# Turning q and k in 32x32 blocks on VectorE, and sink-attention rows in pairs

## The chip, the core and the metric

The kernel runs on one core of one Trainium2 chip. The time is the device time of one execution in microseconds; the figure used is the median of several executions. A profile is one further execution, recorded instruction by instruction. PE is the matrix engine (TensorE), DVE the VectorE, ACT the ScalarE, POOL the GpSimd; SP issues the transfers.

## The reference

Two attention layers follow each other, in float32. Shapes: 4 batches, 8 heads, 768 positions, head size 64.

```python
# first layer: every row sees the 4 first keys (sinks) and a window of 128
scores = scale * np.matmul(q, k.transpose(0, 1, 3, 2))
keep = is_sink | in_window
scores = np.where(keep, scores, -1e9)
a = softmax(scores);  x = (a @ v) -> [B, S, 512]
# second layer: four experts, causal attention each, top 2 of 4 by a gate
logits = x @ w_gate
for e in range(4):
    q, k, v = x @ wq[e], x @ wk[e], x @ wv[e]
    a = softmax(causal(scale * q @ k.T))
    out += gate_weight[e] * ((a @ v) @ wo[e])
```

`setup_inputs` draws q, k, v and the weights at random, with 4 sinks and a window of 128.

## The kernel before

The 768 positions are 6 blocks of 128. Work comes in units. A *first* unit is one batch and one pair of heads of the sink attention (`first`, then `band_rows`): 16 of them. A *second* unit is one batch and one pair of experts (`second`, then `wide_rows`): 8 of them. `values` makes the experts' values and the gate of a batch, `store` the output projection.

Every float32 operand of a large product is split into a high part (rounded to the fp32r type) and a low part (the rest), and each product is three matmuls: high·high, high·low, low·high.

A first unit goes as follows.

- q, k and v of two heads are loaded with positions on partitions (`load`, L712, two transfers for each tensor). The rings "qn" and "kn" have two buffers each.
- PE transposes q and k block by block into PSUM (`tr`, L729, 12 transposes of 128x128 per unit). `Pair.put` makes the parts: ACT copies the high part (L404), DVE subtracts for the low part (L408). q is scaled by -1/8 there. k's tile has 132 columns to a block: 128 keys, and 4 columns that repeat the sink keys, written by extra small instructions at L404 and L408.
- For each row block i, `scores` (L432) makes 260 columns for each of the two heads: the 128 keys of the block before, 4 sinks, the 128 keys of the block itself. The heads use the two halves of PE's rows. Each head has a PSUM bank of its own ("s", four buffers of one bank).
- For each head DVE adds a mask and takes the minimum of each row in one instruction (L632, the scores are negative-scaled, so the minimum is the largest score); ACT takes the exponential and the sum (L637); DVE adds 1e-9 and takes the reciprocal (`factor`, L468 and L469).
- In rows 2 to 5, POOL multiplies the sink columns by the factor (`keep`, L648), adds the two halves of the window into 128 columns, for in each row the halves hold complementary keys (`merge`, L656), and multiplies by the factor (`norm`, L663). Rows 0 and 1 are only multiplied.
- PE transposes the probabilities of two rows (L510; L486 for rows 0 and 1), DVE and ACT copy them out (L513 with a triangular mask, L356 or L358), and PE multiplies by the values (L453), by value differences and by the sinks (L457).

The order of all this is not the order of the code. Each piece is a `Step` with a priority, a cost by engine and what it waits for; `Plan.emit` places the steps one by one in a simulated time and emits the instructions in that order, so each engine's queue is fixed in advance. Priorities come from the place of the unit in a written list (`ORD` for a batch, `LAST` for the last: a number is a first unit of the batch, p a second unit of the batch before, c one of its own) and from leads and lags (`LEAD_S`, `PREP_1`, `AV_LAG` and others). `STAY` is a penalty on PE for changing between full-array, row-tiled (scores) and column-tiled (values) work.

Of the kernel before, what the change touches and what calls it, by code (L numbers as in the profile page):

```python
# [11 lines left out]
F32R = mybir.dt.float32r  # L12
AF = mybir.ActivationFunctionType
OP = mybir.AluOpType
# [15 lines left out]
STAY = 45.29  # L30
# [31 lines left out]
class Plan:  # L62
# [7 lines left out]
    def step(self, prio, cost, fn, after=(), new=(), use=(), fifo=None, moves=0, mode="full", behind=()):  # L70
        s = Step(prio, cost, fn, after, new, use, moves, mode, behind)
        if fifo is not None:
            self.fifo.setdefault(fifo, []).append(s)
        self.steps.append(s)
        return s
# [74 lines left out]
def kernel(  # L150
# [27 lines left out]
    none_kept = n_sink == 0 and window == 0  # L178

# [7 lines left out]
             "gate": 2, "gates": 1, "st": 6, "s": 4, "t": 3, "acc": 1}  # L187
# [21 lines left out]
    def window_mask(m, off, sinks):  # L209
        nc.gpsimd.affine_select(out=m, in_=m, pattern=[[-1, 128]], compare_op=OP.is_ge,  # L210
                                fill=-NEG, base=off, channel_multiplier=1)
        nc.gpsimd.affine_select(out=m, in_=m, pattern=[[1, 128]], compare_op=OP.is_ge,
                                fill=-NEG, base=window - 1 - off, channel_multiplier=-1)
# [6 lines left out]
    if banded:  # L220
        for i, ns in ((0, n_sink), (1, n_sink), (2, 0)):
            m = consts.tile([128, RW], F32, name=f"bmask{i}")
            nc.gpsimd.memset(m, 0.0)
            if i:
                window_mask(m[:, :128], 128, ns)
                if i == 1 or n_sink < 4:
                    nc.gpsimd.memset(m[:, 128 + (0 if i == 1 else n_sink):SW], -NEG)
            window_mask(m[:, SW:], 0, 0 if i else ns)
            for ii in range(i, NB if i == 2 else i + 1):
                row_mask[ii] = m  # L230

        own = consts.tile([128, 128], F32, name="own")
# [17 lines left out]
    else:  # L250
        for i in range(NB):
# [7 lines left out]
            if not none_kept:  # L259
                for c, j in enumerate(seen[i]):  # L260
# [5 lines left out]
                            compare_op=OP.is_ge, fill=-NEG, base=0, channel_multiplier=1)  # L266

    st_ring = [consts.tile([128, 5, 2], F32, name=f"st{n}") for n in range(rings["st"])]
# [93 lines left out]
    class Pair:  # L362
# [25 lines left out]
        def put(self, which, lo, hi, ps, t, prio, mul, after, kept=None):  # L388

            use, n, x = [t, self.tile(which)], (hi - lo) * 128, self.tile(which)  # L390
            sinks = which and self.ext and lo == 0
            if which == 0:
                cs = slice((lo - self.lo) * 128, (hi - self.lo) * 128)
                pieces = [(ps, lambda a: x.t[:, a, cs])]
            else:
                pieces = [(lambda: ps().rearrange("p (j c) -> p j c", c=128),
                           lambda a: self.k_at(x.t[:, a, :], slice(lo, hi), slice(0, 128)))]
                if sinks:
                    pieces.append((lambda: ps()[:, None, :4].to_broadcast([128, self.nk - 1, 4]),
                                   lambda a: self.k_at(x.t[:, a, :], slice(0, self.nk - 1), slice(128, SW))))  # L400

            def high():
                for src, dst in pieces:
                    nc.scalar.activation(dst(0), src(), AF.Copy, scale=mul)  # L404

            def low():
                for src, dst in pieces:
                    nc.vector.scalar_tensor_tensor(dst(1), src(), mul, dst(0).bitcast(F32), op0=OP.mult, op1=OP.subtract)  # L408
            some = 70 if sinks else 0
            h = plan.step(prio, {ACT: some + 60 + 0.833 * n}, high, after, (), use)  # L410
            steps = [h, plan.step(prio, {DVE: some * 1.3 + 70 + 1.04 * n}, low, [h], (), use)]
            if which and kept is not None:

                if sinks:
                    self.kept = plan.step(prio, {DVE: 70}, lambda: nc.vector.tensor_copy(kept, x.t[:, :, :4]), steps[:], (), [x])
                elif lo == self.k0:
                    def place():
# [540 lines left out]
```

## Time and profile before

| | |
|---|---|
| median of 3 runs | 441.64 us (440.98 to 441.94) |
| span of the profiled execution, first to last instruction | 438.3 us |
| that execution's own time | not listed apart from the three runs |
| mean granted clock of PE | 0.995 |
| transfers | 28.23 MB in 86,332 packets, 82,912 of them under 512 B |

The span leaves out what lies before the first and behind the last instruction. Engines work side by side, so their busy times do not add up; a busy share says how full an engine is, and the chain of work that ended last says which engine's work set the time. In a line of the groups there are: line of the code, engine, operation, output and inputs, shapes, count, then busy time in us, mean of one in ns, and the idle time just before them with what ended it.

### The profile page before, as it was taken

Reading aid. Unit: us, or ns where it says so; the run is one execution under the profiler, and the core shown is the slowest. Engines: PE = TensorE matmul, PEld = TensorE weight load, DVE = VectorE, ACT = ScalarE, POOL = GpSimd, SP = SyncE. Lnnn points to the kernel's source line nnn. Section 1 sums busy time; section 2 is a strip of 40 time slices with the busy share of each in tenths; the row PEclk is TensorE's granted clock in tenths of the full one; section 3 lists DMA queues with packets and bytes.
Section 4 is the critical chain, followed back from the end, with each engine's and each line's share of the span. In section 5 each row is a group of like instructions: output and inputs, shape, how many; then the busy total and the mean of one; then the engine's idle time right before and its main releaser. Section 6 shows DMA issues by size and latency. Waiting matters only on the chain.

```text
span 438.3 us, 11835 instructions
## 1 busy us (share of the span) xinstructions
PE 425.2 (97%) x4020; PEld 359.5 (82%) x4020; DVE 327.3 (75%) x1323; ACT 294.6 (67%) x910; POOL 271.1 (62%) x478
## 2 busy tenths in 40 slices
PE   8889999999999999999999999999999999999996
PEld 7568778988888888988888888898788788978874
DVE  3889986797769888559659988866967847455753
ACT  4989995477868868258768966864858747134650
POOL 8989999848638936437656856663655470073550
PEclk9989999999999999999999999999999999999999
DMA  8959771014005334013104426110000000021012
GB/s 169 229 116 180 159 158 38 2 37 109 2 1 110 92 110 126 2 26 83 40 1 82 90 67 173 28 37 1 1 1 2 1 2 1 18 79 50 2 49 97
DMA packets 86332, 28.23 MB, mean 64 GB/s; under 512 B 82912, under 2 KB 82912, under 8 KB 86272
## 3 DMA queue, kind: packets, MB, share of 16 engines
q1 hardware_dynamic: 86272, 27.48, 26.6%
q8 instruction: 32, 0.52, 0.5%
q14 instruction: 28, 0.23, 0.2%
HBM read 21.05 MB, written 6.29 MB: 62 GB/s over the span
## 4 chain that ended last, share of the span: by engine, by line
PE 81%; DVE 9%; ACT 4%; POOL 3%; issue 2%; POOLq 0%; ACTq 0%; DVEq 0%
PE acc L453 16%; PE s L432 15%; PE t L757 14%; PE t L486 11%; PE t L785 8%; PE t L831 8%; PE t L729 3%; PE t L510 3%; DVE p L632 2%; ACT pt L356 1%; PE acc L457 1%; DVE pt L513 1%; DVE p L568 1%; DVE ks L408 1%; PE t L516 1%
## 5 line engine op out<-in xcount | busy, mean ns | idle before, releaser
L637 ACT ACTIVATE p<-p,st 128x260 f32<-128x260 f32 (+1 forms) x192 | 93.6, 494 | 18.8 <-DVE st L632 14.8
L432 PE MATMUL s<-ks,qs 64*128 64x260 f32 (+4 forms) x960 | 92.0, 318 | 1.8 <-DVE st L632 0.8
L585 POOL TENSOR_TENSOR p<-p,st 128x128 f32<-128x128 f32 (+5 forms) x96 | 87.7, 936 | 3.1
L432 PEld LDWEIGHTS s<-ks,qs 64*128 64x128 f32 x960 | 69.1, 187 | 20.4 <-issue 10.4
L663 POOL TENSOR_TENSOR p<-p,st 128x256 f32<-128x256 f32 x96 | 65.4, 688 | 27.8 <-DVE st L469 18.2
L578 ACT ACTIVATE p<-p,st 128x384 f32<-128x384 f32 (+5 forms) x96 | 63.9, 668 | 23.1 <-DVE st L568 19.6
L632 DVE CUSTOM_DVE_ANT_0 p<-s,bmask 128x260 f32<-128x260 f32 (+1 forms) x192 | 69.8, 398 | 6.4 <-PE s L432 5.6
L356 ACT ACTIVATE pt<-t 128x512 f32<-128x512 f32 (+1 forms) x110 | 58.7, 544 | 20.1 <-PE t L486 10.6
L486 PE MATMUL t<-ident,p 128*128 128x128 f32 x432 | 63.2, 281 | 2.3 <-POOL p L663 0.7
L656 POOL TENSOR_TENSOR p<-p 128x256 f32<-128x256 f32 x64 | 46.6, 734 | 27.9 <-ACT p L637 27.5
L486 PEld LDWEIGHTS t<-ident,p 128*128 128x128 f32 x432 | 47.0, 141 | 10.8 <-issue 2.8
L568 DVE CUSTOM_DVE_ANT_0 p<-s,cmask 128x512 f32<-128x512 f32 (+3 forms) x96 | 50.8, 554 | 5.5 <-PE s L432 4.8
L472 POOL TENSOR_TENSOR st<-st,gate 128x2 f32<-128x2 f32 x48 | 9.4, 197 | 66.1 <-DVE st L469 39.2
L408 DVE SCALAR_TENSOR_TENSOR ks<-t,ks 128x384 fp32r<-128x384 f32 (+3 forms) x64 | 27.9, 456 | 19.9 <-ACT ks L404 19.6
L453 PE MATMUL acc<-pt,v 128*64 128x128 f32 x672 | 42.0, 276 | 0.0
L453 PE MATMUL acc<-pt,vn 128*64 128x128 f32 x448 | 40.7, 284 | 0.2 <-DVE x L344 0.2
L453 PEld LDWEIGHTS acc<-pt,v 128*64 128x64 f32 x672 | 36.2, 137 | 4.5 <-issue 2.2
L404 ACT ACTIVATE ks<-t 128x384 fp32r<-128x384 f32 (+3 forms) x64 | 24.8, 417 | 21.9 <-PE t L757 21.6
L637 ACT ACTIVATION_READ_ACCUMULATOR p<-p,st 128x1 f32 x192 | 38.0, 198 | 0.0
L468 DVE TENSOR_REDUCE st<-st 128x2 f32<-128x4 f32 x144 | 22.1, 154 | 20.5 <-ACT p L578 9.1
L785 PE MATMUL t<-wvh,x 128*128 128x260 f32 x192 | 36.7, 286 | 0.5 <-ACT pt L356 0.5
L408 DVE SCALAR_TENSOR_TENSOR qs<-t,qs 128x384 fp32r<-128x384 f32 (+2 forms) x48 | 26.4, 552 | 12.7 <-ACT qs L404 12.5
(103 smaller groups left out, 879.1 us busy)
## 6 DMA issues: line engine op xcount, KB each, us to landing
vn<-in_v_dram SPq DMA_DIRECT2D x32, 192.0 KB, 3.5
out_dram<-o SPq DMA_DIRECT2D x24, 256.0 KB, 2.0
qn<-in_q_dram SPq DMA_DIRECT2D x30, 192.0 KB, 4.3
kn<-in_k_dram SPq DMA_DIRECT2D x30, 192.0 KB, 4.3
o<-in_moe_wo_dram SPq DMA_DIRECT2D x2, 256.0 KB, 4.3
v<-in_moe_wv_dram SPq DMA_DIRECT2D x4, 128.0 KB, 4.1
v<-in_moe_wq_dram SPq DMA_DIRECT2D x4, 128.0 KB
v<-in_moe_wk_dram SPq DMA_DIRECT2D x4, 128.0 KB, 3.8
```

Of the source, the lines that this page charges most:

```text
L356: nc.scalar.activation(dst(), src(), AF.Copy)
L408: nc.vector.scalar_tensor_tensor(dst(1), src(), mul, dst(0).bitcast(F32), op0=OP.mult, op1=OP.subtract)
L432: nc.tensor.matmul(o, self.qs.t[hs, a, qs], self.ks.t[hs, b, ks], start=n == 0, stop=n == 2)
L453: nc.tensor.matmul(o[e * 64:e * 64 + 64], lhs, rhs, start=e not in self.begun, stop=last and i == self.hi - 1)
L486: nc.tensor.transpose(t.t[:, 2 * e + c, :], block(e, c), ident)
L578: nc.scalar.activation(x, x, AF.Exp, bias=st.t[:, 0, es], scale=-1.0, accum_out=st.t[:, 1, es])
L585: nc.gpsimd.tensor_mul(x, x, st.t[:, 2, e:e + 1].to_broadcast([128, n * 128]))
L632: nc.vector.tensor_tensor_reduce(out=p.t[:, e, a:], in0=s.t[:, a:RW], in1=row_mask[i][:, a:], scale=1.0, scalar=BIG, op0=OP.add, op1=OP.mi ...
L637: nc.scalar.activation(x, x, AF.Exp, bias=st.t[:, 0, e:e + 1], scale=-1.0, accum_out=st.t[:, 1, e:e + 1])
L663: nc.gpsimd.tensor_mul(x, x, st.t[:, 2, :][:, :, None].to_broadcast([128, 2, z - a]))
L757: nc.tensor.matmul(ps, w[a][:, c, es], X[b, c].t[:, x, cs], start=c == 0 and m == 0, stop=c == NCH - 1 and m == 2)
L785: nc.tensor.matmul(ps()[:, :VW], X[b, c].t[:, a, qs], W["wv"][w][:, c, :], start=c == 0 and n == 0, stop=c == NCH - 1 and n == 2)
```

## The change

For batches 1 to 3, q and k no longer go through PE. A transfer lays out each 32-column half of a head on 32 partitions, in runs of 32 numbers; DVE then transposes every 32x32 block in place, ACT copies the high part, and POOL subtracts for the low part. Batch 0 keeps PE's transposes. The scaling by -1/8 moves from q into the minimum instruction. The sink columns of k are placed by one POOL instruction for both parts.

In rows 2 to 5 the mask and the merge go. DVE copies, where a triangular predicate holds, the scores of the row's own block over those of the block before, in PSUM, for both heads at once; what remains is 132 columns, and the minimum runs over those with one mask for all these rows. Two rows share one tile of probabilities, one sum and reciprocal, one sink product and one norm. Both heads' scores are one PSUM buffer of two banks (ring "s": two buffers instead of four single ones).

The constants of the plan are set anew, the list of units among them.

```diff
+        def turn(self, which, lo, hi, src, nat, prio, after):
+            x, n = self.tile(which), (hi - lo) * 128
+            new, used = self.fresh(which)
+            part = lambda a: self.part(which, a, lo, hi)
+            turned = plan.step(prio, {DVE: 95 + 1.04 * n}, lambda: nc.vector.transpose(src(), src()), after, (), [nat])
+            h = plan.step(prio, {ACT: 95 + 0.833 * n}, lambda: nc.scalar.activation(part(0), src(), AF.Copy),
+                          [turned], new, [nat] + used, fifo=("qs", "ks")[which] if new else None)
+            def low():
+                nc.gpsimd.tensor_sub(part(1), src(), part(0).bitcast(F32))
...
+            def go():
+                nc.gpsimd.tensor_copy(self.k_at(self.ks.t, slice(0, self.nk - 1), slice(128, SW)),
+                                self.ks.t[:, :, None, :4].to_broadcast([128, 2, self.nk - 1, 4]))
...
+                        if which == 2 or by_pe:
+                            nc.sync.dma_start(t.t[:, a:z, e, :], x.rearrange("(t p) d -> p t d", p=128)[:, a:z, :])
+                            continue
+                        for h in range(2):
+                            to = t.t[64 * e + 32 * h:64 * e + 32 * h + 32].rearrange("p j e d -> p (j e d)")
+                            nc.sync.dma_start(to.rearrange("p (n c) -> p n c", c=32)[:, 4 * a:4 * z, :],
+                                              x.rearrange("(n r) (h c) -> h r n c", r=32, c=32)[h, :, 4 * a:4 * z, :])
...
+            def pick(s2=s2):
+                nc.vector.copy_predicated(s2.t[:, :, :128], earlier.bitcast(I32)[:, None, :].to_broadcast([128, 2, 128]), s2.t[:, :, SW:RW])
...
+                def low(e=e, n=n, s2=s2):
+                    nc.vector.tensor_tensor_reduce(out=p.t[:, n, :], in0=s2.t[:, e, :SW], in1=pair_mask, scale=-scale,
+                                                   scalar=BIG, op0=OP.add, op1=OP.min, accum_out=st.t[:, 0, n:n + 1])
...
-                def merge(p=p):
-                    nc.gpsimd.tensor_add(p.t[:, :, :128], p.t[:, :, :128], p.t[:, :, SW:])
...
+        r = factor(prio - LEAD_N, st, sums, w=4)
...
+        def norm():
+            nc.gpsimd.tensor_mul(p.t[:, :, :128], p.t[:, :, :128], f()[:, :, None].to_broadcast([128, 4, 128]))
...
-             "gate": 2, "gates": 1, "st": 6, "s": 4, "t": 3, "acc": 1}
+             "gate": 2, "gates": 1, "st": 6, "s": 2, "t": 3, "acc": 1}
-STAY = 45.29
+STAY = 32.79
-    LEAD_S, LEAD_E, LEAD_N = 9.9, 3.89, 4.91
-    WIDE_S, WIDE_E, WIDE_N = 10.54, 0.28, 6.11
-    UNIT_1, UNIT_2, AV_LAG = 11.19, 19.96, 4.12
+    LEAD_S, LEAD_E, LEAD_N = 11.81, 7.88, 6.72
+    WIDE_S, WIDE_E, WIDE_N = 10.9, 4.23, 6.32
+    UNIT_1, UNIT_2, AV_LAG = 12.14, 21.17, 7.72
-    ORD = "0 1 p0 2 p1 3"
-    LAST = "0 1 2 p0 3 p1 c0 c1"
+    ORD = "0 1 p0 p1 2 3"
+    LAST = "0 1 p0 3 2 p1 c0 c1"
-    PREP_0, PREP_1, PREP_2, VALUES, STORE = 11.25, 15.12, 10.77, 11.53, 6.72
-    WP, WS, LOAD_0, PREP_3, VALUES_0 = 11.14, 15.74, 34.09, 9.97, 11.15
+    PREP_0, PREP_1, PREP_2, VALUES, STORE = 19.49, 7.91, 17.67, 18.4, 13.2
+    WP, WS, LOAD_0, PREP_3, VALUES_0 = 10.42, 20.53, 37.8, 10.0, 11.15
```

More of the change, by code (lines that the diff above doesn't have):

```diff
@@ L409, in put @@
[L409 to L417, printed above, removed]
-                        copy = nc.vector.tensor_copy if to.eng == DVE else nc.gpsimd.tensor_copy
-                        copy(self.k_at(x.t, slice(self.k0, self.k0 + self.nk - 1), slice(128, SW)),
-                             kept[:, :, None, :].to_broadcast([128, 2, self.nk - 1, 4]))
-                    to = plan.step(prio, {DVE: 110, POOL: 220}, place, [h] + self.source, (), [x])
-                    steps.append(to)
@@ new lines, in turn_by_pe, with tr @@
+        def turn_by_pe(self, which, lo, hi, src, nat, prio, after):
+            t = new_t()
+            def tr():
+                for j in range(hi - lo):
+                    nc.tensor.transpose(t.t[:, j, :], src()[:, j, :], ident)
+            new, used = self.fresh(which)
+            tt = plan.step(prio, {PE: 109 * (hi - lo)}, tr, after, [t] + new, [nat] + used,
+                           fifo=("prep", ("qs", "ks")[which]) if new else "prep")
+            self.put(which, lo, hi, lambda: t.t[:, :hi - lo, :].rearrange("p c n -> p (c n)"), t, prio, [tt])
@@ L507, in tr @@
         def tr():
-            for r, p in enumerate(ps):
-                for e in range(2):
-                    nc.tensor.transpose(t.t[:, 2 * r + e, :], p.t[:, e, :128], ident)
-        tt = plan.step(prio, {PE: 436}, tr, normed, [t, whole, part], ps)
+            for n in range(4):
+                nc.tensor.transpose(t.t[:, n, :], p.t[:, n, :128], ident)
+        tt = plan.step(prio, {PE: 436}, tr, normed, [t, whole, part], [p])
         flat = lambda x: x.t.rearrange("p r e n -> p (r e) n")
@@ L549, in wide_rows @@
                 c1 = min(c0 + 4, n)
-                ss = [buf("s", [128, 512]) for _ in range(2)]
+                s2 = buf("s", [128, 2, 512])
                 runs = []
@@ L695, in over, with first @@
         return [x for a, b, steps in ready if a < hi and b > lo for x in steps]
-    def first(b, hp, groups, prio_of, prep_prio, load_prio, kept):
-        lo, hi = groups[0][0], groups[-1][1]
-        pair = Pair(banded, lo, hi)
-        whole = (b, hp, lo) == (0, 0, 0) and hi > 3
+    def first(b, hp, groups, prio_of, prep_prio, load_prio):
+        pair = Pair(banded)
+        whole, by_pe = (b, hp) == (0, 0), b == 0
         nat, loaded = [], []
@@ L714, in first @@
                 before = [x[2][0] for x in loaded[-1]]
                 loaded[-1].append((a, z, [plan.step(
-                    load_prio + (0.1 if n else 0.2 if which == 2 else 0), {SP: 950}, load, (), [] if n else [t], [t] if n else [],
-                    moves=364 * (z - a), behind=before, fifo=None if n else tag)]))
-        pair.source = KEPT.get(hp, []) if kept is not None else []
-        cuts = {w: [(a, min(a + 3, hi)) for a in range(lo if w == 0 else pair.k0, hi, 3)] for w in range(2)}
@@ L735, in first @@
-        if kept is not None and lo == 0:
-            KEPT[hp] = [pair.kept]
-        value = (lambda j, e: nat[2].t[:, j - pair.k0, e, :], lambda js: loaded[2][0][2], [nat[2]], pair.k0)
+                    load_prio + (0.1 if n else 0.2 if which == 2 else 0), {SP: 950 if which == 2 or by_pe else 1900}, load, (), [] if n else [t],
+                    [t] if n else [], moves=364 * (z - a), behind=before, fifo=None if n else tag)]))
+        for a, z in cut("0 3 6" if whole else TURNS):
+            for which in range(2):
+                t = nat[which]
+                (pair.turn_by_pe if by_pe else pair.turn)(which, a, z, lambda t=t, a=a, z=z: t.t[:, a:z].rearrange("p j e d -> p j (e d)"), t, prep_prio,
+                          over(loaded[which], a, z))
```

288 lines of the change are left out of this document (133 added, 155 removed).

## The prediction

> **What bounds the kernel now.** I read the page's first part, then the busy time in three stretches, then the chain of work that ended last in the first two of them.
>
> ```profile
> span 438.3 us, 11835 instructions
> PE 425.2 (97%) x4020; PEld 359.5 (82%) x4020; DVE 327.3 (75%) x1323; ACT 294.6 (67%) x910; POOL 271.1 (62%) x478
> ```
>
> ```profile
> core 0: us, PE busy (x) PEld busy (x) DVE busy (x) ACT busy (x) POOL busy (x), PEclk, DMA share, GB/s
> 0.00:60.00 60.00, 53.17 (x484) 42.05 (x484) 48.33 (x222) 50.15 (x174) 54.87 (x122) 0.97 0.81 169
> 60.00:420.00 360.00, 357.91 (x3437) 306.38 (x3436) 271.39 (x1089) 241.54 (x731) 212.87 (x354) 1.00 0.19 46
> ```
>
> The next two lines are the chain by line, of the stretch 60 to 420 us and of 0 to 60 us.
>
> ```profile
> by line: PE acc L453 19.0%; PE s L432 17.9%; PE t L757 17.1%; PE t L486 12.4%; PE t L785 9.8%; PE t L831 7.2%; PE t L729 3.5%; PE t L510 3.3%; PE acc L457 1.7%; issue 1.3%; DVE p L568 1.2%; PE t L516 0.9%; ACT pt L356 0.7%; DVE pt L513 0.6%
> ...
> by line: DVE p L632 10.2%; issue 9.1%; DVE pt L513 6.5%; PE s L432 5.3%; ACT pt L356 5.2%; DVE ks L408 5.0%; ACT p L637 4.7%; DVE x L344 3.7%; PE t L486 3.5%; DVE qs L408 3.4%; DVE pt L358 2.7%; ACT ks L404 2.7%; POOL p L663 2.6%; POOL bmas
> ```
>
> A busy PE proves little by itself, since its spans overlap; the chain does. From 60 to 420 us the PE entries add up to 92.8% of it (19.0+17.9+17.1+12.4+9.8+7.2+3.5+3.3+1.7+0.9), so a nanosecond of PE work taken out there is worth about a nanosecond. The other engines have room (DVE 271 of 360 us, POOL 213). The first 60 us are another regime: VectorE heads the chain, and POOL (54.9 of 60), ACT (50.2) and DVE (48.3) are all nearly full, because batch 0's four sink-attention units have no projections beside them. A cut of PE work there is worth nothing, and any DVE work added there is worth its price.
>
> **PE: what leaves.** The transposes of q and k are L729, 192 in all, of which batches 1 to 3 hold 12 pairs x 12 = 144. The second fence is the transposes by stretch; the third has pieces of the chain (start, duration, count).
>
> ```profile
> L729 PE MATMUL t<-ident,qn 128*128 128x128 f32 x96 | 16.8, 286 | 1.6 <-ACT pt L356 1.1 <-DVE pt L513 0.5
> L729 PE MATMUL t<-ident,kn 128*128 128x128 f32 x96 | 16.5, 282 | 0.1
> ```
>
> ```profile
> 0.00:60.00 60.00, 12.52 (x72) 9.02 (x72) 0.97 0.81 169
> 60.00:420.00 360.00, 16.79 (x120) 13.78 (x120) 1.00 0.19 46
> ```
>
> ```profile
> 105.87 0.87 PE t L486 x8
> ...
> 132.52 1.01 PE t L729 x9
> ```
>
> The mean of 286 ns is latency. Eight transposes that follow other full-array work occupy the chain for 0.87 us, 109 ns each; nine of L729 take 1.01 us, 112 ns each. So 120 x 0.109 = 13.1 us leave the stretch where PE is the chain (its 3.5% of 360 us, 12.6 us, says the same); the other 24 (2.6 us) leave the first 60 us and I count them at nothing. Scores, projections and P·V keep their matmuls.
>
> **DVE: what leaves and what comes.**
>
> ```profile
> L632 DVE CUSTOM_DVE_ANT_0 p<-s,bmask 128x260 f32<-128x260 f32 x160 | 62.6, 421 | 3.1 <-PE s L432 2.4
> L632 DVE CUSTOM_DVE_ANT_0 p<-s,bmask 128x128 f32<-128x128 f32 x32 | 8.7, 283 | 3.3 <-PE s L432 3.2
> L468 DVE TENSOR_REDUCE st<-st 128x2 f32<-128x4 f32 x144 | 22.1, 154 | 20.5 <-ACT p L578 9.1 <-ACT p L637 7.1 <-POOL p L656 1.9
> L469 DVE RECIPROCAL st<-st 128x2 f32<-128x2 f32 x144 | 23.9, 166 | 5.0
> L408 DVE SCALAR_TENSOR_TENSOR qs<-t,qs 128x384 fp32r<-128x384 f32 x32 | 17.6, 550 | 6.2 <-ACT qs L404 6.1
> L408 DVE SCALAR_TENSOR_TENSOR ks<-t,ks 128x20 fp32r<-128x20 f32 x16 | 2.7, 169 | 0.0
> L358 DVE COPY v<-t 128x256 f32<-128x256 f32 x18 | 7.6, 423 | 12.2 <-PE t L785 11.9 <-POOL p L656 0.3
> L358 DVE COPY pt<-t 128x512 f32<-128x512 f32 x35 | 23.7, 686 | 5.2 <-PE t L486 5.1
> ```
>
> Rows 2 to 5 of 16 pairs are 64 rows, so 128 masked minima shrink from 260 to 132 columns: 128 x (421-283) = -17.7 us. Two rows share one sum and reciprocal: -32 x (154+166) = -10.2. The 20-column sink copies go: -2.7. The low parts of 48 q/k groups go: -48 x 0.55 = -26.4. New are 48 in-place block transposes of 128x384, of which the trace has none. Their bounds are 0.42 us (the 256-column copy, if reading SBUF were much quicker) and 1.1 us (two passes of 0.55); I take one pass, 0.55, the row of the same size: +26.4 (20 to 53). New too are 64 predicated copies of 2x128 columns from PSUM to PSUM: 0.42 us if source and destination stream together (the 256-column copy), 0.69 if the old destination is streamed as well (the 512-column copy). I take 0.42, because only one side carries new data: +27.1 (to +43.9). The sum is -3.5 us, at worst +40, on 327. In the steady stretch that is hidden under PE; it costs wherever first-attention units stand side by side, since there DVE's order is minimum, factor and evacuation in one queue, and PE's next scores wait for a score tile to be freed. That tile now covers two banks, and both heads wait for the pick.
>
> The Trainium skill speaks against moving a transpose to this engine: by "VectorE: DVE Perf Modes", section "The three transpose paths", VectorE turns 32x32 blocks only and a 128x128 turn of bf16 takes 311 ns there. At 3 x 311 ns a group would take an estimated 0.93 us and the DVE sum would be about +15 us instead of -3.5; no run so far shows the instruction.
>
> **ACT and POOL.**
>
> ```profile
> L637 ACT ACTIVATE p<-p,st 128x260 f32<-128x260 f32 x160 | 81.1, 513 | 15.9 <-DVE st L632 12.0 <-POOL p L663 1.8 <-DVE gate L813 1.6
> L637 ACT ACTIVATE p<-p,st 128x128 f32<-128x128 f32 x32 | 12.6, 398 | 2.9 <-DVE st L632 2.9
> L656 POOL TENSOR_TENSOR p<-p 128x256 f32<-128x256 f32 x64 | 46.6, 734 | 27.9 <-ACT p L637 27.5
> L663 POOL TENSOR_TENSOR p<-p,st 128x256 f32<-128x256 f32 x80 | 48.7, 615 | 8.9 <-ACT p L637 5.0 <-PE t L486 3.5
> L648 POOL TENSOR_TENSOR psk<-p,st 128x24 f32<-128x24 f32 x64 | 14.2, 226 | 2.2 <-DVE st L469 1.4 <-DVE st L468 0.4
> L585 POOL TENSOR_TENSOR p<-p,st 128x512 f32<-128x512 f32 x16 | 16.4, 1046 | 0.2
> L585 POOL TENSOR_TENSOR p<-p,st 128x384 f32<-128x384 f32 x16 | 12.9, 828 | 0.5
> ```
>
> ACT: 128 exponentials lose 115 ns each, -14.7 us. POOL: the 64 merges go, -46.6; 64 sink products become 32, -7.2; 64 norms of 256 become 32 of 512, 33.5 for 39.4, -5.9. POOL gets 48 subtractions of 128x384, between 0.83 us (the product of that size) and 1.10 (1.5 times the merge, which reads two whole tiles); I take 1.0: +48. The 16 sink placements, 40 elements each, are nearest to the sink product: 16 x 0.23 = +3.7. Sum -8 us on 271. The k low part now waits in POOL's queue behind norms that PE's transposes wait for; 4 x 1.0 us per unit is covered as long as the preparation runs ahead.
>
> **The start.**
>
> ```profile
> 0.00:60.00 60.00, 11.64 (x16) 0.97 0.81 169
> ...
> 0.00:60.00 60.00, 20.26 (x110) 0.97 0.81 169
> ```
>
> The first line is the merges (L656), the second the minima (L632). In 0 to 60 us POOL loses 11.6 of merges, some 3 in norms and sink products, and gains 8 low parts (two pairs of batch 1): -7. ACT loses some 40 x 0.115 = 4.6. DVE stays level: 20 picks cost 8.4, 40 narrower minima and 10 factors save 8.7. The chain there is mostly DVE, so I take only -1 us, with +5 as the other end (the pick at 0.69 us adds 20 x 0.27 = 5.4) and -6 if POOL and ACT were the true holders.
>
> **DMA.** q and k of batches 1 to 3 come in runs of 32 numbers, 128 B instead of 256 B: twice the packets, 6144 per pair instead of 3072, from eight DMAs instead of four. The page of DMA for 100 to 120 us:
>
> ```profile
> DMA packets 4707, 1.22 MB, mean 61 GB/s; under 512 B 4704, under 2 KB 4704, under 8 KB 4704
> ...
> q1 hardware_dynamic: 4704, 1.18, 26.9%
> ...
> SPq L712 <- PE t L729: 95.0, 11, 28.3
> ```
>
> 26.9% of 16 engines x 20 us is 86 us for 4704 packets: 18.3 ns each. If a packet of half the size costs as much, a pair's q and k take 6144 x 18.3 / 16 = 7.0 us instead of 3.5; if the bytes decide, still 3.5. With a DMA share of 0.19 after 60 us this is hidden; in the first 60 us (0.81) two pairs add up to 7 us of transfers, which have some 11 us of empty DMA time there. The third line is SP's queue: loads already wait 95 us in all for L729 to give q/k buffers back, so they are issued as early as buffers allow. The buffer now goes free after POOL's low part, perhaps 3 us later per group.
>
> The Trainium skill, "DMA: Bandwidth & Descriptors", section "Why small descriptors are slow (HBM only)", gives a packet about 3 fixed cycles beside one per 32 B, so 11 cycles for 256 B and 7 for 128 B. From the measured 18.3 ns that is an estimated 11.6 ns, and 4.5 us per pair. Either way the transfer is hidden.
>
> **The sum.** 438.3 - 13.1 - 1 = 424.2 us of span. The median of the runs shown, 441.64, is 3.3 us above this span, and I keep that: 427.5. PE gets some waits back as it becomes faster than its feeders, and the order written out anew moves things both ways; I call it 427.
>
> **The rivals.**
> 1. *A larger gain, 420.* POOL and ACT hold the start, so it loses 6 us, and the 2.6 us of its PE transposes count in part: 441.6-13.1-6-2 = 420. For: POOL at 54.9 of 60 us. Against: DVE entries lead that chain.
> 2. *DVE takes over half, 436.* The pick at 0.69 us and the turn at 1.1: DVE +40 us, 367 in all. The start loses 5.4 us, and of the 13.1 PE gives back some 6 in waits for score tiles: 441.6-13.1+5.4+2 (turns of the first two pairs) = 436, up to 442. For: two PSUM operands in one instruction occur nowhere in this trace. Against: no DVE row here exceeds one pass.
> 3. *Slower, 448: the pick paces the first-attention units.* It sits between scores and minimum, and holds a two-bank score tile of which there are two. At a cost of 1.0 us, 0.58 over mine, 64 of them add 37 us to DVE; half of it on the path (the start, and the runs of first units, which the new order makes four long: 2, 3, 0, 1) is 18.5, so 441.6-14.1+18.5 = 446, and 2 for the turns. It decides from about 0.86 us a pick on, where half of 64 x 0.44 eats the 14.1 us.
> 4. *Loads come late, 445.* Each of the eight DMAs writes 32 partitions. Were only a quarter of the engines used, a pair's q and k would take 6144 x 18.3 / 4 = 28 us, and with two buffers each, four first units in a row at some 13 us each (55 minima in the first 60 us, 12 to a unit) would stand still some 6 us a batch, 18 in all: 441.6-14.1+18 = 445. It decides once a pair's load passes about 18 us. Against: the 256-byte loads already fill 0.81 of all 16 engines in the first 60 us.
>
> **How the numbers follow.** Forecast 0.52, larger gain 0.14, DVE half 0.21 (a quarter of it within 0.2% of before or above), pick 0.08, loads 0.05. The forecast's own range is 422 to 432 (the pick's and the turn's inner bounds, and the start from -3 to +3); the range for 8 in 10 runs from 416 to 438 and leaves out the two slower cases and the tail of the third. A measurement tells about 0.2% (0.9 us) from no change. Faster 0.82, same 0.05, slower 0.13.
>
> **What would show it.** The transposes' PE group falls to 48; the 60-to-420 chain stays over 90% PE, and that stretch's work ends 13 us sooner. The predicated copy at about 0.42 us, the block transpose at 0.55, POOL's subtraction at 1.0; POOL near 263 us, ACT near 280, DVE near 324. Packets rise by 36,864. I am wrong if a DVE row is above 0.7 us for the pick, if PE waits for DVE or for loads add up to more than 10 us after 60 us, or if the first units of batch 0 take longer than before.

## The result, and the profile after

The changed kernel takes 434.47 us (median of 4, 433.79 to 435.18) against 441.54 us (440.98 to 441.94) of the kernel before, run beside it: a ratio of 0.9842, 95% interval 0.9825 to 0.9858. It is faster by 7.1 us, a little less than half of the 14.5 us that were forecast. The profiled span fell from 438.3 to 432.4 us.

The page of the changed kernel: busy times, the granted clock in 40 slices, packets, and the chain of work that ended last.

```profile
span 432.4 us, 11450 instructions
PE 413.8 (96%) x3876; PEld 342.9 (79%) x3876; DVE 321.1 (74%) x1307; ACT 281.7 (65%) x894; POOL 265.0 (61%) x413
PEclk9699999999999999999999999999999999999999
...
q1 hardware_dynamic: 123904, 27.48, 30.1%
...
PE 72%; DVE 12%; ACT 5%; POOL 5%; issue 3%; DMA 2%; SPq 0%; POOLq 0%; DVEq 0%; ACTq 0%
```

The same two lines of the kernel before:

```profile
PEclk9989999999999999999999999999999999999999
...
PE 81%; DVE 9%; ACT 4%; POOL 3%; issue 2%; POOLq 0%; ACTq 0%; DVEq 0%
```

The side engines came out within 3 us of the forecast (DVE 321.1 for 324, ACT 281.7 for 280, POOL 265.0 for 263). What moved is the chain: PE holds 72% of it instead of 81%, and DVE, ACT, POOL, issue and DMA have taken 9 points more. The groups of the changed kernel, by line and shape, show that the price of each new instruction was right:

```profile
L703 DVE CUSTOM_DVE_ANT_0 p<-s,pair_mask 128x132 f32<-128x132 f32 x128 | 32.6, 287 | 0.5
L696 DVE COPY_PREDICATED s<-earlier,s 128x256 f32<-128x256 int32 x64 | 25.5, 421 | 1.4 <-PE s L463 1.4
L451 POOL TENSOR_TENSOR qs<-qn,qs 128x384 fp32r<-128x384 f32 x24 | 24.2, 1013 | 16.2 <-ACT qs L447 16.2
L446 DVE STREAM_TRANSPOSE kn<-kn 128x384 f32<-128x384 f32 x24 | 13.2, 562 | 0.1
L446 DVE STREAM_TRANSPOSE qn<-qn 128x384 f32<-128x384 f32 x24 | 12.8, 557 | 0.1
L434 PE MATMUL t<-ident,kn 128*128 128x128 f32 x24 | 4.8, 318 | 1.0 <-DVE ks L411 1.0
L434 PE MATMUL t<-ident,qn 128*128 128x128 f32 x24 | 4.5, 298 | 0.1
```

A pick takes 0.421 us (0.42 forecast), a turn 0.56 (0.55), GpSimd's low part 1.01 (1.0), and 48 transposes are left on PE. So the missing 7.4 us are not in a price. Two views say where to look. First the chain of the changed kernel from 60 to 420 us, by line, where the kernel before had 92.8% PE:

```profile
by line: PE t L794 17.2%; PE acc L484 16.5%; PE s L463 14.6%; PE t L517 11.0%; PE t L822 10.0%; PE t L868 6.8%; PE t L540 2.8%; issue 1.9%; PE acc L488 1.6%; DVE p L598 1.5%; DVE pt L543 1.4%; DVE pt L365 1.2%; ACT p L608 1.2%; ACT pt L363 
```

The PE entries that can be seen add up to 80.5%. Then the busy times of the two stretches:

```profile
0.00:60.00 60.00, 50.35 (x472) 39.66 (x474) 46.35 (x209) 47.37 (x165) 49.92 (x104) 0.94 0.82 162
60.00:420.00 360.00, 355.11 (x3353) 296.99 (x3350) 270.20 (x1092) 233.60 (x729) 215.06 (x310) 1.00 0.22 48
```

PE still looks 98.6% busy after 60 us (355.11 of 360), because the spans of matmuls overlap and short waits vanish inside them. To see those waits I counted from the starts of the matmuls in the trace: each at the distance at which its kind follows itself when packed (109 ns for a transpose, columns divided by 2.4 plus 8 to 14 ns for longer ones, half of it where two share the array), 94 to 149 ns for each change between full-array, row-tiled and column-tiled work, and the rest, time at half clock included, as waiting. By this estimate, in us from the first matmul to the last:

| kernel | packed PE work | changes of tiling | waiting | of it after 60 us |
|---|---|---|---|---|
| before | 368.0 | 33.2 | 31.9 | 15.3 |
| changed | 352.3 | 34.9 | 39.6 | 21.2 |
| difference | -15.7 | +1.7 | +7.7 | +5.9 |

15.7 us of PE work went out, as 144 x 0.109, and 9.4 us came back as waits and changes: -6.3 us, which is the fall of the span (5.9) with 0.4 us more ahead of the first matmul and behind the last. The experiments ask what these waits are.

### The profile page after: what moved, and what is told of

Same layout as the page of the kernel before. It is cut to its first block, busy times and chain, and to the rows that moved or that the text cites. A ratio compares the mean times of both kernels' runs of the same rounds, so it can differ in the third digit from the quotient of the medians.

```text
span 432.4 us, 11450 instructions
## 1 busy us (share of the span) xinstructions
PE 413.8 (96%) x3876; PEld 342.9 (79%) x3876; DVE 321.1 (74%) x1307; ACT 281.7 (65%) x894; POOL 265.0 (61%) x413
## 4 chain that ended last, share of the span: by engine, by line
PE 72%; DVE 12%; ACT 5%; POOL 5%; issue 3%; DMA 2%; SPq 0%; POOLq 0%; DVEq 0%; ACTq 0%
PE acc L484 15%; PE t L794 14%; PE s L463 13%; PE t L517 10%; PE t L822 8%; PE t L868 6%; PE t L540 3%; ACT pt L363 2%; DVE pt L543 2%; PE acc L488 1%; DVE p L598 1%; DVE p L703 1%; DVE s L696 1%; DVE pt L365 1%; ACT p L608 1%
## 5 line engine op out<-in xcount | busy, mean ns | idle before, releaser
L608 ACT ACTIVATE p<-p,st 128x128 f32<-128x128 f32 (+5 forms) x96 | 63.6, 664 | 18.5 <-DVE st L598 16.3
L707 ACT ACTIVATE p<-p,st 128x132 f32<-128x132 f32 x128 | 50.5, 398 | 12.3 <-DVE st L703 10.5
L365 DVE COPY pt<-t 128x512 f32<-128x512 f32 (+1 forms) x54 | 32.0, 596 | 7.5 <-PE t L517 7.2
L716 POOL TENSOR_TENSOR psk<-p,st 128x48 f32<-128x48 f32 x32 | 8.6, 268 | 43.3 <-DVE st L500 31.9
L868 PE MATMUL t<-woh,y 128*128 128x512 f32 x96 | 34.7, 412 | 0.0
L451 POOL TENSOR_TENSOR qs<-qn,qs 128x384 fp32r<-128x384 f32 x24 | 24.2, 1013 | 16.2 <-ACT qs L447 16.2
L722 POOL TENSOR_TENSOR p<-p,st 128x512 f32<-128x512 f32 x32 | 33.4, 1042 | 0.1
L703 DVE CUSTOM_DVE_ANT_0 p<-s,pair_mask 128x132 f32<-128x132 f32 x128 | 32.6, 287 | 0.5
L794 PE MATMUL t<-x,wqh 128*128 128x256 f32 (+1 forms) x128 | 32.7, 344 | 0.0
L794 PE MATMUL t<-x,wkh 128*128 128x256 f32 (+1 forms) x128 | 32.1, 340 | 0.4 <-DVE qs L411 0.4
```

The lines of the kernel that those rows point to most:

```text
L608: nc.scalar.activation(x, x, AF.Exp, bias=st.t[:, 0, es], scale=-1.0, accum_out=st.t[:, 1, es])
L703: nc.vector.tensor_tensor_reduce(out=p.t[:, n, :], in0=s2.t[:, e, :SW], in1=pair_mask, scale=-scale, scalar=BIG, op0=OP.add, op1=OP.min, a ...
L707: nc.scalar.activation(p.t[:, n, :], p.t[:, n, :], AF.Exp, bias=st.t[:, 0, n:n + 1], scale=-1.0, accum_out=st.t[:, 1, n:n + 1])
L794: nc.tensor.matmul(ps, w[a][:, c, es], X[b, c].t[:, x, cs], start=c == 0 and m == 0, stop=c == NCH - 1 and m == 2)
L868: nc.tensor.matmul(ps(), Y[b, c].t[:, a, qs], W["wo"][w][:, c, :], start=c == 0 and n == 0, stop=c == EP - 1 and n == 2)
```

## The experiments

Theory one: behind PE stands a second path, only a few us shorter, and less PE work uncovers it. Rivals: one part of the change is dearer than it looks, the new order is bad, or the loads are late.

**Less and more PE work, nothing else changed.** In the kernel before, batches 1 to 3 make one of three q and k transposes and use its result three times (e1); then they make each of them twice (e5).

```diff
-                    for j in range(a, z):
+                    for j in range(a, z if b == 0 else a + 1):      # e1_pe_light
+                    for j in [x for x in range(a, z) for _ in range(2 if b else 1)]:   # e5_pe_heavy
```

> The kernel before, with its order untouched, but in batches 1 to 3 only one of three q/k transposes is made and its result is copied three times (96 of 144 transposes left out, the numbers of q and k in those batches are not the right ones). Nothing is added to any engine. 80 of the 96 lie past 60 us: 80 x 0.109 = 8.7 us of PE work. Theory A (past 60 us PE time is worth its length; the changed kernel loses the rest because VectorE, GpSimd and the loads got new work): 441.5 - 8.7 = 433, at most 434.5. Theory B (in an order fixed ahead, PE meets the softmax path of other engines again and again, so freed PE time mostly turns into waits whatever is added): 437 to 440.

Measured: 438.68 us against 441.38, ratio 0.9944 (0.9925 to 0.9964). Of the 10.5 us taken out, 2.7 are had.

> The kernel before, order untouched, but each of the 144 q/k transposes of batches 1 to 3 is made twice into the same place (15.7 us more PE work, the same numbers; 13.1 us of it past 60 us). The mirror of the run that took 96 of them out and gained 2.5 us of 8.7. If PE is the slowest path with only a thin margin over the next one, adding is not symmetric to taking away: 441.4 + 13.1 = 454.5, at least 452. If the gain was small because PE time there simply lies in gaps of the order, adding should cost as little as taking away gained: 444 to 446.

Measured: 454.14 us against 441.61, ratio 1.0277 (1.0251 to 1.0303). Of 15.7 us put in, 12.5 are paid. The chains by engine, first of e1, then of e5:

```profile
PE 77%; DVE 13%; ACT 5%; issue 3%; POOL 1%; ACTq 0%; POOLq 0%; DVEq 0%
```

```profile
PE 86%; DVE 5%; POOL 4%; ACT 2%; issue 2%; POOLq 0%; ACTq 0%; DVEq 0%
```

Up, a nanosecond of PE work costs 0.8; down, it is worth 0.26. If only the transposes past 60 us are counted, 13.1 us put in and 8.7 taken out, the figures are 0.95 and 0.31. In the count above e1's waiting rises from 31.9 to 39.6 us, as much as in the changed kernel. This needs none of the new instructions. It is what a second path of nearly the same length does; which work makes up that path, these two runs do not show.

**Is it only the order?** An order written for longer PE work might hide the gain. e13 gives the work of e1 constants searched for it, e10 gives the kernel before new constants and nothing else.

```diff
-                tt = plan.step(prep_prio, {PE: 109 * (z - a)}, tr, ...
+                tt = plan.step(prep_prio, {PE: 109 * (z - a if b == 0 else 1)}, tr, ...   # e13_light_tuned
-    LAST = "0 1 2 p0 3 p1 c0 c1"
+    LAST = "0 2 1 p0 3 p1 c0 c1"                                     # e13 and e10_before_tuned
-    PREP_0, PREP_1, PREP_2, VALUES, STORE = 11.25, 15.12, 10.77, 11.53, 6.72
+    PREP_0, PREP_1, PREP_2, VALUES, STORE = 12.56, 15.25, 9.91, 15.32, 6.78   # e10; leads and lags likewise
```

> e1_pe_light's work (the kernel before, in batches 1 to 3 one of three q and k transposes, its result used three times), but the planner is told of the shorter TensorE step and the constants are searched anew for it. Theory one (behind TensorE stands a second path, only a few us shorter, whatever the order): new constants add at most 2 us to e1's gain, 436.5 to 438.5 us. Theory two (only the order, written for the longer work, hides the rest of the 10.5 us): with an order of its own the gain comes nanosecond for nanosecond, 431 to 433 us.

> The kernel before with none of the change's work, its constants of the schedule searched anew by the same planner (the plan grows shorter by 0.74 us of 428.7). Theory one (the new work made room that new constants then use; constants alone give the old work nothing): within 1 us of the kernel before, 440.5 to 442. Rival (the kernel before was merely badly scheduled, and any new order gives those 7 us): 435 to 437 us.

Measured: e13 440.73 us against 441.63, ratio 0.9981 (0.9969 to 0.9992); e10 442.55 against 441.94, ratio 1.0017 (1.0 to 1.0033). Theory two of e13 falls: an order made for the lighter work brought less on the chip than e1's old order. Theory one gave 436.5 to 438.5 and missed too, on the other side. Constants alone give the old work nothing.

**The parts alone, and the parts with the old constants.** e2 has only the turn, GpSimd's low parts and the 128-byte loads, e11 only the picked rows in pairs; e3 is the whole change with the old constants and list.

```diff
+                if b:                                                # e2_turn_before, in the kernel before
+                    pair.turn(which, a, z, ...)
+                    continue
-        whole, by_pe = (b, hp) == (0, 0), b == 0
+        whole, by_pe = (b, hp) == (0, 0), True                       # e11_rows_before, and the old constants
-    ORD = "0 1 p0 p1 2 3"
+    ORD = "0 1 p0 2 p1 3"                                            # e3_old_consts; all other constants likewise
```

> The kernel before with only the turn of q and k on VectorE, low parts on GpSimd and the 128 B loads (scale moved into the minimum as in the changed kernel); rows single, merges kept, constants and list of units as before. PE loses 15.7 us, GpSimd gains some 52 us (48 x 1.01 + 16 x 0.22) and stands near 320 of 440. Theory A: PE's 13.1 us come out less what GpSimd takes back, 430 to 436. Theory B: 436 to 442, no better than half of the 13.1 us. A third, that GpSimd's extra 52 us are what the row pairs had to pay for: slower than before, over 442.

> The kernel before with the picked rows and the row pairs alone: every batch's q and k are turned by TensorE and split as before, the loads are the old ones, and the constants are the old ones. VectorE then gets the 64 copies of 0.42 us and the 2 x 132 minimum in place of 260 wide ones on top of its old low parts. Theory one (a pick on the way from scores to exponentials costs its latency, and VectorE, relieved of no low parts, queues): slower than before by 4 to 10 us, 446 to 452. Rival (the shorter minima, exponentials and paired row ends are the part that pays, and the turn adds nothing): 434 to 438 us.

> The changed kernel with the constants and the list of units of the kernel before (units 0 1 p0 2 p1 3, leads, lags and the mode penalty as before). All work is the changed kernel's. Theory A (work sets the time): within 2 us of 434.5. Theory B (the order sets how much of the freed PE time is kept): 438 to 443, the larger part of the 7 us gone.

Measured: e2 457.12 us against 441.38, ratio 1.0364 (1.0324 to 1.0403); e11 451.64 against 441.94, ratio 1.0224 (1.018 to 1.0269); e3 441.54 against 441.38, ratio 1.0001 (0.9979 to 1.0024). Busy times, first of e2, then of e11:

```profile
PE 425.3 (93%) x3876; PEld 351.8 (77%) x3876; DVE 337.2 (74%) x1315; ACT 290.4 (64%) x894; POOL 317.4 (69%) x538
```

```profile
PE 431.3 (96%) x4020; PEld 360.5 (80%) x4020; DVE 324.8 (72%) x1313; ACT 280.4 (62%) x888; POOL 219.5 (49%) x365
```

POOL is the last number: 271 us in the kernel before, 317 with the turn alone, 219 with the pairs alone. Each part alone, with the old constants, makes the kernel slower by 10 to 16 us. For e2 a part of this can be seen in the trace: a small gate instruction on DVE (the three times are its shortest, median and longest, in ns), and PE's wait behind it.

```profile
L842 DVE TENSOR_TENSOR gates<-gate x4: 246/249/8710, 95.0 to 399.4; 128x96 f32<-128x96 f32 x4
```

```profile
105.83 0.48 PE L459 MATMUL s<-ks,qs 64*128 64x128 f32 x2 [5.79 <-ACT ks L405]
```

The instruction took 8.71 us instead of 0.25 once, from 94.98 to 103.69 us, while GpSimd worked 8.60 us of these 8.71; the gate, a copy of k on ACT and PE's next scores stood behind it, and PE waited 5.79 us. That GpSimd's work held it up was not tested. e2 also spends six to eight stretches of 3.41 us at half clock, the kernel before one to four (the last section has the price). What makes e11 slow was not shown: its DVE is busy 324.8 us, no more than the 327.3 of the kernel before. Together the parts come out even, and the new constants bring the 7 us. With the old constants no part has a gain of its own; constants searched for one part alone were not tried.

**Other orders of the changed kernel.** e7 has other constants with the same unit list, e8 other constants and lists. In e8 three first units stand side by side between batches 1 and 2, where the changed kernel has four, but five between batches 2 and 3.

```diff
-    LEAD_S, LEAD_E, LEAD_N = 11.81, 7.88, 6.72
+    LEAD_S, LEAD_E, LEAD_N = 11.38, 7.35, 6.13                       # e7_order_a; others likewise
-    ORD = "0 1 p0 p1 2 3"
+    ORD = "0 1 p0 3 p1 2"                                            # e8_order_b; others likewise
-    LAST = "0 1 p0 3 2 p1 c0 c1"
+    LAST = "1 0 2 3 p0 p1 c0 c1"                                     # e8_order_b
```

> The changed kernel with the same instructions and the same list of units; only constants of the plan differ (leads, lags, places, the mode penalty, and two costs of the plan set to what the trace measured: GpSimd's low part 1.0 us, the sink placement 0.22), so the instructions stand in another order on each engine. If the order decides how much of the 15.7 us is kept, another order moves the time by several us with all work unchanged, and this one was chosen to be tighter: 429 to 433. If the work decides, within 1 us of 434.5.

> As the run before, with other constants and the units listed as 0 1 p0 3 p1 2, in the last batch 1 0 2 3 p0 p1 c0 c1: all four first units of the last batch stand side by side, while elsewhere no more than three do. If the order decides: 429 to 434. If the work decides: within 1 us of 434.5. If runs of four first units are the weak place, it is no slower than the order before it.

Measured: 434.12 us (ratio 0.9833, 0.9807 to 0.9859) and 434.77 us (0.9836, 0.981 to 0.9862), both the same as the changed kernel. Three orders that differ much end within 0.7 us of each other; the old constants (e3) end 7 us later with the same work.

**The suspects, one at a time.** All in the changed kernel's own order: the block transposes left out (e4), the predicated copies left out (e6), the old 256-byte loads (e12, with as many transfers as the changed kernel, so it tests the size of the packets alone).

```diff
-            turned = plan.step(prio, {DVE: 95 + 1.04 * n}, lambda: nc.vector.transpose(src(), src()), after, (), [nat])
+            turned = plan.step(prio, {DVE: 95 + 1.04 * n}, lambda: None, after, (), [nat])        # e4_no_turn
-                nc.vector.copy_predicated(s2.t[:, :, :128], earlier.bitcast(I32)[:, None, :].to_broadcast([128, 2, 128]), s2.t[:, :, SW:RW])
+                return                                                                              # e6_no_pick
-                            nc.sync.dma_start(to.rearrange("p (n c) -> p n c", c=32)[:, 4 * a:4 * z, :], ...
+                            nc.sync.dma_start(t.t[:, js, e, :], x.rearrange("(t p) d -> p t d", p=128)[:, js, :])   # e12_plain_load
```

> The changed kernel in its own order, but the 48 block transposes on VectorE are left out (q and k of batches 1 to 3 go on unturned, so the numbers are not the right ones): VectorE loses 48 x 0.56 = 27 us. Theory A with the turns as the cost: 434.5 falls by 5 to 8 us, to 427 to 429. Theory B: PE does not wait for the turns but for order and latency: 432 to 434.5.

> The changed kernel in its own order without the 64 predicated copies (the own block's scores are not brought over, so the probabilities are not the right ones). VectorE loses 64 x 0.42 = 27 us, as much as without the turns (which gave 0.7 us), but this time on the path from scores to exponential. If the softmax path of single rows is what PE waits for: 434.5 falls by 3 to 6 us. If PE waits for no single operation but for the order as a whole: 433 to 434.5.

> The changed kernel in the same order, but q and k of batches 1 to 3 are fetched in the old 256-byte rows instead of 128-byte pieces: half as many packets there, two issues in place of four. The block transposes then leave q and k not transposed as the products need them; all times of other instructions stay. Theory one (the loads lie behind other work): within 0.5 us of the changed kernel, 434.0 to 435.0 us. Rival (packets compete with the moe loads, and issues on SP delay later ones): 1 to 3 us faster, 431.5 to 433.5 us.

Measured: e4 433.75 us (ratio 0.9833, 0.9797 to 0.9869), e6 431.02 (0.9768, 0.9744 to 0.9793), e12 434.94 (0.9851, 0.9806 to 0.9896). Without the turns DVE is busy 301.8 us instead of 321.1, without the picks 301.7: the same 19 us, but the turn is worth 0.7 us, which is within the spread of both kernels' runs, and the pick 3.5; the smaller packets cost nothing that can be seen. So it is not DVE's load but the place that counts: the pick stands between a row's scores and its exponential. It also holds the score tile for longer; which of the two costs the time was not separated. The exponentials' group, in the changed kernel and then in e6; the last numbers are ACT's idle time before them:

```profile
L707 ACT ACTIVATE p<-p,st 128x132 f32<-128x132 f32 x128 | 50.5, 398 | 12.3 <-DVE st L703 10.5 <-DVE st L499 1.4
```

```profile
L707 ACT ACTIVATE p<-p,st 128x132 f32<-128x132 f32 x128 | 50.5, 399 | 6.8 <-DVE st L703 6.1 <-DVE st L499 0.4
```

**The start.** In the changed kernel the four sink keys of batch 0 too are placed by GpSimd, and there its copy (L422) stands behind the building of masks. The timeline of the changed kernel (start, duration, in brackets the idle time and who ended it):

```profile
9.68 0.29 POOL L272 TENSOR_SCALAR_AFFINE_SELECT cmask<-cmask 128x128 f32<-128x128 f32 x1
9.92 0.11 POOL L280 MEMSET tril<- 128x16 f32 x1
...
10.09 0.22 POOL L281 TENSOR_SCALAR_AFFINE_SELECT tril<-tril 128x16 f32<-128x16 f32 x1
...
10.26 0.22 POOL L422 CAST ks<-ks 128x40 fp32r<-128x40 f32 x1
...
10.53 0.99 PE L463 MATMUL s<-ks,qs 64*128 64x260 f32 x12 [1.98 <-POOL ks L422]
```

e9 lets VectorE place them in batch 0, in the same order of everything; e15 is e9 with constants searched anew.

```diff
-                nc.gpsimd.tensor_copy(self.k_at(self.ks.t, slice(0, self.nk - 1), slice(128, SW)),
+                (nc.gpsimd if self.sink_pool else nc.vector).tensor_copy(self.k_at(self.ks.t, slice(0, self.nk - 1), slice(128, SW)),
...
-        pair = Pair(banded)
+        pair = Pair(banded, sink_pool=b > 0)
```

> The changed kernel, the same instructions in the same global order, but in batch 0 alone VectorE instead of GpSimd places the four sink keys behind the band (line 422): there GpSimd's copy stands behind its mask building, and TensorE waits 1.98 us for it at 10.5 us. Theory one (the first 60 us run on one path, and what is taken out of it is had at the end): the wait falls to what VectorE's 0.56 us low part at 8.63 us leaves, some 0.5 us, and the end comes 1.3 to 1.6 us earlier: 432.9 to 433.2 us, ratio about 0.981 to the kernel before. Theory two (a second path of much the same length bounds the end too): under 0.5 us of it is left, 434.0 to 434.5 us.

> e9_sink_dve's instructions with constants and unit lists searched anew (plan 2.1 us shorter). Theory one (orders of this work end at one floor, as e7 and e8 did): within 0.8 us of e9's 432.35, 431.6 to 433.2 us. Rival (a better order is still to be had): 429.8 to 431 us.

Measured: e9 432.35 us (432.12 to 432.61) against 441.94, ratio 0.9791 (0.9759 to 0.9824); e15 432.74, ratio 0.9803 (0.9783 to 0.9822). e9 is 2.1 us below the changed kernel and the fastest version here that computes all of it. But the reason expected for it holds only in part. Its page and its timeline:

```profile
PEclk9999999999999999999999999999999999999999
```

```profile
9.69 0.98 PE L464 MATMUL s<-ks,qs 64*128 64x260 f32 x12 [1.30 <-DVE st L668]
```

The products start 0.84 us sooner, not 1.5. The rest fits the clock: the profiled execution of the changed kernel runs PE at half clock for two stretches of 3.41 us after this wait, that of e9 for none. In all their executions it is two or three against none or one, and the last section prices a stretch at about 0.7 us. e15's new constants add nothing that can be seen, but its executions had two to four such stretches, so its order may be the better one.

**Do the pieces add up?** e14 has e4, e6 and e9 in one.

```diff
-            turned = plan.step(prio, {DVE: 95 + 1.04 * n}, lambda: nc.vector.transpose(src(), src()), after, (), [nat])
+            turned = plan.step(prio, {DVE: 95 + 1.04 * n}, lambda: None, after, (), [nat])
-                nc.vector.copy_predicated(...)
+                return
+        pair = Pair(banded, sink_pool=b > 0)
```

> The changed kernel in its order, with three things together that e4, e6 and e9 had one at a time: the 48 block transposes left out (q and k of batches 1 to 3 stay unturned), the 64 predicated copies left out (rows 2 to 7 keep the masked scores), and batch 0's sink keys placed by VectorE. Theory one (each stood on a stretch of its own of the path that ends last): their gains of 0.7, 3.5 and 2.1 us add up, 427.7 to 428.8 us, which is about what had been forecast for the change with all its parts. Theory two (they shorten one and the same waiting): little more than the largest two, 429.5 to 431 us.

Measured: 430.76 us, ratio 0.9754 (0.9739 to 0.9768). They don't add up: 0.7 + 3.5 + 2.1 would be 6.3, and 3.7 are had, e6's gain and 0.3. But the clock accounts for most of what is missing: all four executions of e14 spend three stretches at half clock where e9 had none or one, an estimated 1.9 us of the 2.6. So e14 does not show that one waits behind the other.

**How far down does it go?** In the changed kernel's order, e16 leaves out one of three partial products of every score, e17 half of the columns of GpSimd's normalising products, e18 both.

```diff
-            for n, (a, b) in enumerate(THREE):
+            for n, (a, b) in enumerate(THREE[:2]):                   # e16_two_products, e18_two_half
-            nc.gpsimd.tensor_mul(p.t[:, :, :128], p.t[:, :, :128], f()[:, :, None].to_broadcast([128, 4, 128]))
+            nc.gpsimd.tensor_mul(p.t[:, :, :64], p.t[:, :, :64], f()[:, :, None].to_broadcast([128, 4, 64]))   # e17_half_norm, e18; L615 likewise
```

> The changed kernel in its order, with two of the three partial products in every score (320 of 960 matmuls of line 463 left out, so the scores lack the product of q's low part with k's high part): by the matmuls' packed lengths 21 us of TensorE work. No other instruction changes. Theory one (behind TensorE stands a second path a few us shorter): the end comes 3 to 7 us earlier, 427.5 to 431.5 us. Theory two (TensorE still bounds most of it): 12 us or more, 422 us or less.

> The changed kernel in its order, with GpSimd's normalising products of lines 615 and 722 on half of their columns (the other half of the weights stays unnormalised): some 55 of GpSimd's 265 us go out, and each row's way from exponentials to transposes becomes 0.2 to 0.7 us shorter. No TensorE work changes. Theory one (the second path is the rows' way, and GpSimd's products are a link of it): 2 to 4 us earlier, 430.5 to 432.5 us. Rival (GpSimd has the time, what stands on the path is ahead of it, between scores and exponentials): within 0.8 us of the changed kernel, 433.7 to 435.3 us.

> e16 and e17 together: two of three products in every score, and the normalising products on half of their columns. If TensorE alone bounds, it ends where e16 does; if GpSimd's products are the second path, 4 us or more ahead of e16; if the second path lies elsewhere, within 1.5 us of e16.

Measured: e16 428.54 us (ratio 0.9723, 0.9693 to 0.9754), e17 431.96 (0.9795, 0.9768 to 0.9823), e18 425.18 (0.9643, 0.962 to 0.9667). 21.3 us less of packed PE work give 5.9 us, and the waiting grows from 39.6 to 54.5. 49 us less of GpSimd's (265.0 to 216.4) give 2.5, and beside e16 3.4, just between the bounds that were set for "the second path" and "elsewhere". The page of e16, its busy times and its chain:

```profile
PE 398.3 (94%) x3556; PEld 323.2 (76%) x3556; DVE 320.4 (75%) x1307; ACT 281.2 (66%) x894; POOL 264.3 (62%) x413
...
PE 56%; DVE 22%; ACT 8%; POOL 6%; issue 5%; DMA 2%; SPq 0%; POOLq 0%; DVEq 0%; ACTq 0%
```

The clock differs here too: three to five half-clock stretches in e16, one or two in e17, three in e18, two or three in the changed kernel. At 0.7 us each, e16's gain would be an estimated 7 us at the clock of the changed kernel and e17's 1.8. With PE still "94% busy", 44% of e16's chain is elsewhere. GpSimd's products are one link of what stands behind PE, the pick another. Which links make up the rest was not settled: no single engine or instruction that was taken out gave more than some 0.3 us for each us.

## Why the prediction was right and wrong

**The direction and the prices: right.** Faster, and inside 416 to 438, but outside the forecast's own 422 to 432. The minima, the exponentials, POOL's sum, the pick, the turn and the low parts cost what their rows said. The Trainium skill's "VectorE: DVE Perf Modes", section "The three transpose paths", led to an estimate of 0.93 us for a turn of 128x384; the trace has 0.56 us, so here the measurement decides against the three passes that I read out of it, and a turn takes the 0.55 us of one pass. So rivals 2 and 3, which rested on dearer picks and turns, did not happen as mechanisms, although the time lies near rival 2's 436 (a sum that leaves out the 6 us of waits that its text names; with them it is 442).

**The transfers: right.** e12 shows that the 128-byte packets cost nothing in time. The page of 100 to 120 us of the changed kernel prices them:

```profile
DMA packets 14115, 2.00 MB, mean 100 GB/s; under 512 B 14112, under 2 KB 14112, under 8 KB 14112
...
q1 hardware_dynamic: 14112, 1.97, 58.9%
```

0.589 x 16 x 20 us over 14,112 packets is 13.4 ns each, for a mix of both sizes, against 18.3 before. That is near the 11.6 ns that I had estimated for the small ones from "DMA: Bandwidth & Descriptors", section "Why small descriptors are slow (HBM only)", in the Trainium skill; bytes count, not packets alone. Rival 4 did not occur.

**The failed step: "a nanosecond of PE work taken out there is worth about a nanosecond".** It was read from 92.8% of PE in the chain between 60 and 420 us, and it carried 13.1 of the 14.1 us of the sum. The chain names what ended last at each step; it does not say by how much. e1 measured the term alone, without any new instruction: 0.26 us for each us, where e5 measured 0.8 in the other direction. For the 15.7 us that left, the span shows 5.9. Of the signs that I had named, waits of PE for DVE or loads above 10 us after 60 us didn't show: the profile's list has 3.1 us of PE waiting for DVE there, since the waits are many and short (the count has 21.2 us of all kinds there, 5.9 more than before). The chain of over 90% PE did fail: it fell to some 80%. What the second path consists of stays open beyond the two links that e6 and e17 show.

**The pick as "hidden under PE": wrong.** Its price was right and its place was not weighed to the end. The prediction said that it costs where first units stand side by side; e6 measured 3.5 us in all. Whether the time is lost in those places was not shown: e8, with a shorter run of them in one place, is no faster, but it has a longer one in another.

**The start: -1 us forecast, wrong in sign.** The step that failed is the sink placement, priced at 16 x 0.23 us of POOL's time, with no term for who waits for it. In batch 0 it was moved into POOL's queue behind the mask building, where PE waits 1.98 us for it. e9 shows 2.1 us for undoing it, clock included. So the third sign of being wrong, first units of batch 0 that take longer, did show: in the traces the last of their score products starts at 49.1 us instead of 46.9, and in e9 at 47.3.

**What lies around the span.** The 3.3 us that I kept are 2.1 in the result (434.47 less 432.4), 1.2 us to the good: the profiled execution of the kernel before had one stretch of half clock, while most of its executions have two or three.

## What to carry to other kernels

A chain of over 90% on one engine says what sets the end now, not what a cut is worth: test it by taking work out and by putting the same kind of work in, and if only the second shows, look for a second path close behind. Count the stretches at half clock in both kernels before a difference of 1 or 2 us is explained in another way. In a written order, weigh each new instruction by whether it stands between one row's stages (the pick, 3.5 us) or beside them (the turn, at most 0.7 us), not by its busy time. When a small step changes engines, look at what stands ahead of it in that engine's queue at the start, where no other work covers the wait.

## What the runs showed of the hardware

**The clock.** PE's granted clock falls to one half in stretches of 3.41 us or multiples of it, in most profiled executions within the first 40 us alone, apart from the last few us of the span, behind the last matmuls. The time at half clock is (1 - mean clock) x span x 2. The 59 executions of the kernel before that ran beside the experiments, grouped by the number of such stretches, have these means: one 440.11 us (9 executions), two 441.19 (14), three 441.83 (26), four 442.17 (10), a slope of about 0.7 us for each. This accounts for more than half of the variance between its executions; that other kernels pay the same price is an estimate. What comes ahead of it, in the changed kernel and then in e9:

```profile
6.00:12.00 6.00, 3.00 (x29) 2.10 (x27) 3.14 (x11) 2.75 (x9) 5.37 (x21) 1.00 1.16 233
12.00:18.00 6.00, 5.50 (x30) 4.26 (x29) 5.07 (x27) 4.88 (x19) 3.85 (x8) 0.50 1.01 214
```

```profile
6.00:12.00 6.00, 3.97 (x38) 2.85 (x36) 4.16 (x18) 3.69 (x13) 5.37 (x21) 1.00 1.22 238
12.00:18.00 6.00, 4.75 (x43) 3.56 (x42) 5.46 (x25) 5.21 (x21) 4.73 (x7) 1.00 1.09 213
```

With PE busy 3.00 of 6 us the next 6 us ran at 0.50, with 3.97 of 6 at full clock. The Trainium skill's "TensorE: Matmul & The Clock Gate", section "What's actually happening", has half clock after an idle window of some 3.4 us. The trace agrees with the length; but PE was half busy here, and in the last 3.41 us before the drop busy 1.47 us with no pause longer than 1.98, so partial idleness is enough. What decides was not measured, and the busy share alone may not: in e10 the clock fell at 13.06 us, after 3.41 us of which PE was busy 2.51.

**Two PSUM operands in one instruction.** The predicated copy from PSUM to PSUM takes 0.421 us for 256 columns, as a plain copy of 256 columns does (0.423): the destination that stays costs no second pass.
